# Coarse keys of pairs 12 to 31 held as 126 and 18, the left keys of two pairs handled together

## The chip, the cores and the metric

One NeuronCore of a Trainium2 chip runs the whole program. The metric is the device time of one execution in microseconds, the median of several runs. PE is TensorE, which multiplies matrices; DVE (VectorE), ACT (ScalarE) and POOL (GpSimd) do elementwise work; SP (SyncE) issues most of the transfers. Each engine works through its own instructions in the order in which the program was built.

## What is computed

Eight batches, eight heads, 576 positions, 64 features a head. Attention runs at two scales and the sum of both goes through a gated convolution block:

```python
q_d, k_d, v_d = mean of each 4 neighbouring positions of q, k, v   # 144 coarse positions
out_d  = softmax(q_d k_d^T / 8) v_d                                # coarse attention
out_up = repeat(out_d, 4)
out_local = softmax over |i - j| < 4 of (q k^T / 8), times v       # local attention
x    = out_up + out_local           # [8, 576, 512]
gate = sigmoid(causal depthwise conv of x over 5 positions)
y    = (gate * (x @ w_val)) @ w_out
```

## The kernel before

A **pair** is two heads of one batch on 128 partitions; there are 32, four to a batch, and pair p belongs to batch p // 4. For each pair the coarse part has these steps, each an operation of a planner: `sd` (PE, coarse scores, two pairs at once from pair 8 on), `cmx`, `cbi` (DVE), `cexp` (ACT, exponentials and row sums, into the tile `pd` of 112 query rows x 3 groups x 144 keys), `cgrd`, `crcp` (DVE, the tile `crs` of reciprocals), `cnorm` (multiply `pd` by `crs`, on DVE, POOL or ACT as the planner chooses), `tc0` and `tc1` (PE, lines 948 to 956: the keys are cut in two halves of 72; each half is three transposes of 112 x 72 into a PSUM tile), `pdt0` and `pdt1` (ACT, line 959, copies of these into `pdt`), `odp` (PE, lines 1010 to 1027: two halves x two heads, each a matmul of 72 keys by 64 features over 144 columns, added in PSUM) and `od` (ACT, line 1031, the copy of the result, each value twice). The coarse values come as a sum of four transfers into the tile `vs` of a batch: the first is issued by SP, the three that add to it by POOL, each behind the landing of the one ahead of it.

The local part has `sl` (scores), `mx`, `sub`, `exp`, `sum`, `rcp`, `norm` (tile `pexp`), `tl0`, `tl1` (transposes), `pt`, and `x` (PE, local values). `xt` (DVE) adds both scales into the tile `xt`; `xh`, `xl` split it in two parts for the projections, and four `tap` steps (DVE, line 1070) and `gate` make the convolution gate. The projections go in blocks of 504 positions: `v` (PE, tile `val`), `h` (DVE), `hhi`, `hlo` (the split of h, tile `hhl`), `o` (PE, tile `out`), `ob` (ACT, the scaled copy) and a store by SP. A piece of a projection is three matmuls of 504 columns (lines 1159 to 1161).

The order is made by a planner (`Planner.simulate`) from a hand-written order for PE (`ORDER` up to about pair 12, then the pattern `DOUBLE` for two pairs at a time), durations, and due times; it also decides which engine takes `cnorm`, `norm` and the splits. With `DOUBLE` the even pair's and the odd pair's `odp` stand together, then both `x`, then `tl` of the next pair. PSUM tiles of the kind `t` (for `tl`, `tc`, `odp`) have two buffers. `send` (line 644) holds every SP transfer back until the transfer four ahead of it has landed (`PACE = 4`). `keep_warm` (line 627) puts filler matmuls where the planner expects PE to wait.

Of the kernel before, what the change touches and what calls it, by code (L numbers as in the profile page):

```python
# [86 lines left out]
ROWS, NG, GR = 112, 3, 48  # L87


def scored(p):  # L90

    return p if p < TWOS else p - p % 2
# [104 lines left out]
class Planner:  # L197
# [55 lines left out]
    def switch(self, a, b):  # L253

        a, b = ("P" if "." in k[0] else k[0].rstrip("0123456789") for k in (a, b))
        a, b = self.SHAPE[a], self.SHAPE[b]
# [258 lines left out]
def named(text):  # L515

    name, _, n = text.rpartition(".")
    return name, int(n)


def tensor_order(np_):
# [10 lines left out]
    seq = [named(n) for n in ORDER.split()]  # L532
# [7 lines left out]
    def some(name, p):  # L540
        key = (name, scored(p) if name == "sd" else p)
        if 0 <= p < np_ and key not in seq:
            seq.append(key)
# [21 lines left out]
def tile_two_scale_attn_gated_conv(  # L565
# [6 lines left out]
    vgr: bass.AP,  # L572
    w_val: bass.AP,
# [25 lines left out]
    xhs, xls = (cpool.tile([P, NC, spot(LASTB * S) + S], F32R, name=n) for n in ("xhs", "xls"))  # L599

# [57 lines left out]
    def sums_in(b):  # L658
        u = bt.setdefault(b, {})

        def first(nm, src, shape):
            def run():
                u[nm] = inp.tile(shape, F32, tag=nm, name=f"{nm}{b}", bufs=VSB if nm == "vs" else 2)
                send(out=u[nm], in_=src[b, 0])
            return run

        def more(nm, src, r):
            def run():
                nc.gpsimd.dma_start(out=u[nm], in_=src[b, r], accum_op=ALU.add)
            return run  # L670

        for nm, src, shape, user, size in (
            ("qs", qkr, [P, NC, 2, SD], "sd", P * NC * 2 * SD * 4),
            ("vs", vgr, [VROWS, NC, 4, D], "odp", VROWS * NC * 4 * D * 4),
        ):
# [3 lines left out]
            if nm == "vs":  # L679
                last = NC - 1 + b - VSB  # L680
                free = [(user, last)] if last < NC else [(user, NC * (last - NC + 1) + c) for c in range(NC)]
            op((f"{nm}0", b), "SP", 620, first(nm, src, shape), free=free, size=size)
# [146 lines left out]
    def coarse_scores(p):  # L829
# [62 lines left out]
        def norm(eng):  # L892
            if eng is nc.scalar:
                for g in range(NG):
                    nc.scalar.mul(s["pd"][:, g], s["pd"][:, g], s["crs"][:, g : g + 1])
                return
            return eng.tensor_tensor(
                out=s["pd"], in0=s["pd"], in1=s["crs"].broadcast_to([ROWS, NG, SD]), op=ALU.mult
            )

# [10 lines left out]
        for g, k in enumerate(exps):  # L911
            op(k, "ACT", 356, exp(g), [("cbi", p)] + exps[:g][:1], free=[("tc0", p - 2), ("tc1", p - 2)])
# [29 lines left out]
    def coarse_transpose(p, kb):  # L942
# [17 lines left out]

        op(
# [45 lines left out]
    def coarse_av(p):  # L1007
        s = st[p]

        def mm():  # L1010
# [24 lines left out]

        op(
# [242 lines left out]

    def cw_in():  # L1280
        send(out=cw_raw, in_=conv_w)
# [13 lines left out]
    for p in range(NP):  # L1295
# [9 lines left out]
        coarse_av(p)  # L1305
        conv_split(p)
# [82 lines left out]
```

## Time and profile before

| | |
|---|---|
| median of 3 runs | 368.58 us (368.21 to 369.27) |
| the profiled execution, its own time | 365.61 us |
| span of its trace | 363.8 us |
| PE busy | 354.8 us, 98% |
| DVE, ACT, POOL busy | 311.5, 244.1, 70.3 us |
| granted clock of PE, mean | 0.999 of full speed |
| from 140 to 310 us: PE, DVE busy of 170 us | 169.52, 160.74 us |

The profile shows one execution. Busy times of different engines overlap, so only what stands on the chain that ended last makes the time. Matmuls of PE overlap one another in the trace: what one costs is read from the distance between the starts of the groups on both sides of it, not from its own duration. A float32 matmul leaves two records in the trace, a transpose one.

### The profile page before, as it was taken

To read this page: it belongs to the slowest core of one execution; us is meant where nothing else is said; L and a number is where in the kernel's file an instruction comes from. 1 tells how busy PE (TensorE), PEld (TensorE's weight loads), DVE (VectorE), ACT (ScalarE), POOL (GpSimd) and SP (SyncE) were. 2 spreads that over 40 slices of the span, in tenths; PEclk is the share of its full clock that TensorE was granted. 3 is DMA by queue.
4 is the path that set the end of the run, shared out by engine and by line. 5 is a ranking of instruction groups with operands and counts; after the bars stand their busy time and mean duration, and the time that the engine had idled before them with its cause. 6 is when DMAs were issued, how large, how long until landed. Compare 5 with 4: busy or idle time off the path is not lost.

```text
span 363.8 us, 14500 instructions
## 1 busy us (share of the span) xinstructions
PE 354.8 (98%) x6233; PEld 286.3 (79%) x6233; DVE 311.5 (86%) x696; ACT 244.1 (67%) x658; POOL 70.3 (19%) x95
## 2 busy tenths in 40 slices
PE   8899999999999999999999999999999999999996
PEld 5678776777877788888888887788878787878995
DVE  4999999999999699999999999999998996870520
ACT  2999998977687658784868577676767685422221
POOL 5013252622131123211312031202100110000000
PEclk9999999999999999999999999999999999999999
DMA  8999989999999977995699869992434012002012
GB/s 278 315 286 307 325 226 212 253 254 262 249 229 272 251 243 206 227 264 194 231 206 245 244 183 250 220 266 86 142 125 133 2 41 82 33 0 90 25 49 82
DMA packets 23152, 69.01 MB, mean 190 GB/s; under 512 B 2864, under 2 KB 8240, under 8 KB 23088
## 3 DMA queue, kind: packets, MB, share of 16 engines
q1 hardware_dynamic: 18192, 50.42, 41.6%
q0 software_dynamic: 4608, 17.50, 26.3%
q8 instruction: 49, 0.80, 1.0%
q10 hardware_dynamic: 288, 0.16, 0.2%
q14 instruction: 15, 0.12, 0.1%
HBM read 58.63 MB, written 9.44 MB: 187 GB/s over the span
## 4 chain that ended last, share of the span: by engine, by line
PE 78%; DMA 10%; ACT 6%; DVE 3%; issue 1%; POOL 0%; DVEq 0%; ACTq 0%; POOLq 0%
PE out L1159 9%; PE out L1161 8%; PE out L1160 8%; PE val L1159 8%; PE val L1161 8%; PE val L1160 8%; DMA vs<-in_vgr 7%; PE odp L1021 6%; PE x L979 5%; PE tl L929 5%; PE sl L772 5%; PE tc L952 5%; PE sd L849 3%; DMA out_t<-ob 2%; PE sl L758 1%
## 5 line engine op out<-in xcount | busy, mean ns | idle before, releaser
L1070 DVE SCALAR_TENSOR_TENSOR gp<-xt,cw,gp 128x576 f32<-128x576 f32 x128 | 103.4, 812 | 3.1 <-ACT gp L1064 2.4
L1159 PE MATMUL val<-xhs,wh_v 128*128 128x504 f32 (+1 forms) x160 | 63.0, 394 | 0.0
L1161 PE MATMUL val<-xls,wh_v 128*128 128x504 f32 (+1 forms) x160 | 59.5, 372 | 0.0
L1160 PE MATMUL val<-xhs,wl_v 128*128 128x504 f32 (+1 forms) x160 | 59.4, 371 | 0.0
L1159 PE MATMUL out<-hhl,wh_o 128*128 128x504 f32 (+1 forms) x144 | 58.6, 407 | 0.1
L1161 PE MATMUL out<-hhl,wh_o 128*128 128x504 f32 (+1 forms) x144 | 54.8, 381 | 0.0
L1160 PE MATMUL out<-hhl,wl_o 128*128 128x504 f32 (+1 forms) x144 | 54.7, 380 | 0.0
L872 ACT ACTIVATE pd<-sd,cbi 112x144 f32<-112x144 f32 x96 | 35.5, 387 | 7.8 <-DVE cbi L865 7.8
L1251 ACT ACTIVATE ob<-out 128x504 f32<-128x504 f32 (+2 forms) x40 | 22.1, 557 | 24.4 <-PE out L1161 15.3
L1207 POOL TENSOR_TENSOR hhl<-h,hhl 128x504 fp32r<-128x504 f32 (+1 forms) x17 | 19.3, 1138 | 98.8 <-ACT pt L934 41.9
L1187 DVE SCALAR_TENSOR_TENSOR h<-gp,val 128x288 f32<-128x288 f32 (+6 forms) x64 | 26.6, 445 | 12.8 <-PE val L1161 12.7
L959 ACT COPY pdt<-tc 72x336 f32<-72x336 f32 x64 | 25.5, 434 | 16.3 <-PE tc L952 16.1
L1201 ACT CAST hhl<-h 128x504 fp32r<-128x504 f32 (+2 forms) x44 | 22.0, 521 | 20.3 <-DVE h L1187 19.6
L1161 PEld LDWEIGHTS val<-xls,wh_v 128*128 128x128 f32 x160 | 30.1, 188 | 5.2
L1159 PEld LDWEIGHTS val<-xhs,wh_v 128*128 128x128 f32 x160 | 30.1, 188 | 4.6 <-issue 0.8
L1160 PEld LDWEIGHTS val<-xhs,wl_v 128*128 128x128 f32 x160 | 30.2, 189 | 3.6
L809 DVE TENSOR_TENSOR pexp<-ex,rs 64x350 f32<-64x350 f32 x61 | 31.6, 518 | 1.3
L1081 ACT ACTIVATE gp<-gp 128x576 f32<-128x576 f32 x32 | 22.2, 694 | 14.1 <-DVE gp L1070 14.1
L934 ACT COPY pt<-tl 128x256 f32<-128x256 f32 (+1 forms) x64 | 25.7, 430 | 8.7 <-PE tl L929 8.4
L1161 PEld LDWEIGHTS out<-hhl,wh_o 128*128 128x128 f32 x144 | 27.1, 188 | 5.5 <-DVE hhl L1207 0.4
L1159 PEld LDWEIGHTS out<-hhl,wh_o 128*128 128x128 f32 x144 | 27.1, 188 | 5.4 <-DVE h L1187 0.5
L1160 PEld LDWEIGHTS out<-hhl,wl_o 128*128 128x128 f32 x144 | 27.2, 189 | 3.4
(97 smaller groups left out, 711.9 us busy)
## 6 DMA issues: line engine op xcount, KB each, us to landing
qk<-in_qk SPq DMA_DIRECT2D x32, 586.0 KB, 6.1
qs<-in_qkr POOLq DMA_DIRECT2D x18, 576.0 KB, 7.7
vw<-in_vw SPq DMA_DIRECT2D x32, 320.0 KB, 5.4
out_t<-ob SPq DMA_DIRECT2D x32, 252.0 KB, 5.2
vs<-in_vgr POOLq DMA_DIRECT2D x21, 320.0 KB, 8.2
qs<-in_qkr SPq DMA_DIRECT2D x6, 576.0 KB, 6.6
vs<-in_vgr SPq DMA_DIRECT2D x7, 320.0 KB, 6.7
raw_v<-in_w_val SPq DMA_DIRECT2D x4, 512.0 KB, 5.5
```

Source lines behind the costliest of these rows:

```text
L809: return eng.tensor_tensor(out=px[r].rearrange("p (m b) k -> p b m k", b=2)[:, :, :, BQ * e : BQ * e + KW], in0=s["ex"][r].rearrange("p (b ...
L872: nc.scalar.activation(out=s["pd"][:, g], in_=s["sd"][:, g], func=AF.Exp, scale=1.0 / 128.0, bias=s["bi"][:, g : g + 1], accum_out=s["csm" ...
L934: nc.scalar.copy(out=s["pt"][:, lo : lo + n], in_=s["tl", u])
L959: nc.scalar.copy(out=s["pdt"][:, kb], in_=s["tc", kb])
L1070: return nc.vector.scalar_tensor_tensor(out=s["gp"], in0=s["xt"][:, k : k + S], scalar=cw[:, c, k : k + 1], in1=s["gp"], op0=ALU.mult, op1 ...
L1081: nc.scalar.activation(out=s["gp"], in_=s["gp"], func=AF.Tanh, scale=0.5)
L1159: nc.tensor.matmul(out=o, lhsT=wh[:, d, col], rhs=his[d], start=d == 0, stop=False)
L1160: nc.tensor.matmul(out=o, lhsT=wl[:, d, col], rhs=his[d], start=False, stop=False)
L1161: nc.tensor.matmul(out=o, lhsT=wh[:, d, col], rhs=los[d], start=False, stop=d == NC - 1)
L1187: nc.vector.scalar_tensor_tensor(out=t["h"][:, cs], in0=st[b * NC + c]["gp"][:, f:e], scalar=1.0, in1=box["o"][:, cs], op0=ALU.add, op1=AL ...
L1201: nc.scalar.copy(out=t["hh"][:, cuts[n]], in_=t["h"][:, cuts[n]])
L1251: nc.scalar.mul(t["ob"][:, cs], box["o"][:, cs], 0.5)
```

## The change

From pair 12 on (`PD = 12`) the 144 coarse keys are cut in 126 (`KM`) and 18 (`KR`) instead of 72 and 72.

- The 126 keys of a pair take three transposes (one operation `tc1`; there is no `tc0`). The 18 left keys of each of the three groups are multiplied by `crs` into a small tile (`crest`, on DVE, POOL or ACT): 54 columns for the even pair, 54 for the odd pair, 18 columns of zeros between. One transpose at the odd pair turns all 126 columns. `pdt` becomes one copy of 126 x 336 for the even pair and of 126 x 448 for the odd pair.
- `odp` is one operation for two pairs. First four matmuls of 126 keys by 64 features over 144 columns; then twelve over 48 columns with 54 rows (partitions 0 to 53, even pair) or 62 rows (64 to 125, odd pair) and 64 features, on the four quarters of the array in turn. It needs both buffers of the kind `t`.
- The weights of those twelve stand in a zeroed tile (`spare`, two of them, cleared once on POOL). In it, three transfers for each pair (SP, 18 rows x 128 floats, 9 KB each, from the summed values) lay the left values at the rows of their group: 60 transfers more.
- The sums of values come in two tiles: 126 rows and 18 rows of 512 floats (before 80 rows of 1024). Per batch that is one SP transfer and three POOL transfers more, for batches 3 to 7.

The core of the diff:

```diff
+KM, KR = 126, 18
+PD = 12
...
     def switch(self, a, b):
 
+        rest = a[0] == "odp" and a[1] >= PD and a[1] % 2
...
+    def spread(p):
+        b, c = divmod(p, NC)
+
+        def dma(i):
+            def run():
+                at = 4 * KR * (p % 2) + KR * i
+                send(
+                    out=vzs[p // 2 % 2][at : at + KR, i].rearrange("k h d -> k (h d)"),
+                    in_=bt[b]["vr"][:, P * c : P * c + P],
+                )
+            return run
+
+        for i in range(NG):
+            op((f"vz{i}", p), "SP", 620, dma(i), [("vr3", b), ("zero", 0)], free=[("odp", p - 3 - p % 2)], size=KR * P * 4)
...
+        def rest(eng):
+            at = (NG + 1) * (p % 2)
+            out, in_ = rts[p // 2 % 2][:, at : at + NG], s["pd"][:, :, KM:SD]
...
-        op(("cnorm", p), either(526, 1000, 910), 0, norm, [("crcp", p)], port=BOTH)
+        op(("cnorm", p), either(*((526, 1000, 910) if p < PD else (470, 890, 860))), 0, norm, [("crcp", p)], port=BOTH)
+        if p >= PD:
+            op(
+                ("crest", p), either(140, 300, 600), 0, rest, [("crcp", p), ("zero", 0)],
+                free=[("tc1", p - 3 - p % 2)], port=BOTH,
+            )
...
+        def mm_wide():
+            s["pdt"] = work.tile([KM, n, ROWS], F32, tag="pdt", name=f"pdt{p}")
+            s["tc", 1] = tp = ps.tile([KM, n, ROWS], F32, tag="t", name=f"tc{p}", bufs=TB)
+            keep_warm(tp.rearrange("p a b -> p (a b)"))
+            for i in range(NG):
+                nc.tensor.transpose(
+                    out=tp[:, i],
+                    in_=s["pd"][:, i, 0:KM],
+                    identity=(ident_s if crossed(p, i) else ident)[0:ROWS, 0:ROWS],
+                )
+            if p % 2:
+                nc.tensor.transpose(out=tp[:, NG], in_=rts[p // 2 % 2].rearrange("p g k -> p (g k)"), identity=ident[0:ROWS, 0:ROWS])
...
+        def mm_wide():
+            for x in (p - 1, p):
+                st[x]["odp"] = ps.tile([P, SD], F32, tag="t", name=f"odp{x}", bufs=TB)
...
+                for h, r in enumerate((LO, HI)):
+                    nc.tensor.matmul(
+                        out=st[x]["odp"][r].rearrange("p (i j) -> p i j", j=GR),
+                        lhsT=vd[:, h],
+                        rhs=st[x]["pdt"][:, 0:NG, 64 * h : 64 * h + GR],
+                        start=True,
+                        stop=False,
+                    )
+            for i in range(NG):
+                for x, k in ((p - 1, slice(0, NG * KR)), (p, slice(64, KM))):
+                    for h, r in enumerate((LO, HI)):
+                        q = 64 * (1 - h if crossed(x, i) else h)
+                        nc.tensor.matmul(
+                            out=st[x]["odp"][r, GR * i : GR * i + GR],
+                            lhsT=vzs[p // 2 % 2][k, i, h],
+                            rhs=s["pdt"][k, NG, q : q + GR],
+                            start=False,
+                            stop=i == NG - 1,
+                        )
```

Because durations and operations change, the planner also orders some work anew, from about pair 8 on. On PE the pieces between the attention steps stay nearly the same; three filler matmuls appear ahead of `tc` of pair 8. `cnorm` goes to DVE 11 times instead of 16, to POOL 5 times instead of once, to ACT 16 times instead of 15; `crest` goes to ACT 12 times, to POOL 5 times, to DVE 3 times. `norm` of pairs 17 and 25 goes from DVE to POOL.

PE at the coarse transposes of pair 15, before: `tc15_1` and `tc15_0` are the two halves, `out2` a piece of the output projection.

```order
L1161 MATMUL out2_1_2990<-hhl2_1_2759,wh_o_98 128x504
L952 MATMUL tc15_1_3025<-ident_s_78,pd15_2801 72x112 x2
L952 MATMUL tc15_1_3025<-ident_77,pd15_2801 72x112
L952 MATMUL tc15_0_3029<-ident_s_78,pd15_2801 72x112 x2
L952 MATMUL tc15_0_3029<-ident_77,pd15_2801 72x112
L1159 MATMUL out2_0_2917<-hhl2_2_2888,wh_o_98 128x504
```

The same place now; `spare1` is the small tile with the left keys of pairs 14 and 15.

```order
L1277 MATMUL out2_1_3018<-hhl2_1_2778,wh_o_98 128x504
L1023 MATMUL tc15_3057<-ident_s_78,pd15_2823 126x112 x2
L1023 MATMUL tc15_3057<-ident_77,pd15_2823 126x112
L1029 MATMUL tc15_3057<-ident_77,spare1_1719 126x112
L1275 MATMUL out2_0_2947<-hhl2_2_2930,wh_o_98 128x504
```

Six transposes have become four (three at an even pair), between the same pieces.

PE at the weighted values of pairs 12 and 13, before, behind a piece of `val2`:

```order
L1161 MATMUL val2_3_2812<-xls_90,wh_v_96 128x504
L1021 MATMUL odp12_2821<-pdt12_2471,vs3_1436 64x144 x4
L1021 MATMUL odp13_2826<-pdt13_2649,vs3_1436 64x144 x4
L979 MATMUL x12_2835<-pt12_2567,vw12_2173 64x58 x20
L979 MATMUL x13_2857<-pt13_2762,vw13_2549 64x58 x20
L929 MATMUL tl14_1_2884<-ident_77,pexp0_80 128x128 x2
```

The same place now:

```order
L1277 MATMUL val2_3_2834<-xls_90,wh_v_96 128x504
L1098 MATMUL odp12_2842<-pdt12_2572,vs3_1257 64x144 x2
L1098 MATMUL odp13_2843<-pdt13_2672,vs3_1257 64x144 x2
L1109 MATMUL odp12_2842<-pdt13_2672,spare0_1717 64x48 x2
L1109 MATMUL odp13_2843<-pdt13_2672,spare0_1717 64x48 x2
L1109 MATMUL odp12_2842<-pdt13_2672,spare0_1717 64x48 x2
L1109 MATMUL odp13_2843<-pdt13_2672,spare0_1717 64x48 x2
L1109 MATMUL odp12_2842<-pdt13_2672,spare0_1717 64x48 x2
L1109 MATMUL odp13_2843<-pdt13_2672,spare0_1717 64x48 x2
L1060 MATMUL x12_2866<-pt12_2589,vw12_2356 64x58 x20
L1060 MATMUL x13_2889<-pt13_2781,vw13_2578 64x58 x20
```

Four matmuls over 144 columns have gone and twelve over 48 have come; what stands ahead and behind is the same.

SP's queue at the stores of block 3, before (`out_t` is the result, `ob3` a block of it):

```order
L644 DMA out_t<-ob3_0_3781 128x504
L644 DMA out_t<-ob3_1_3834 128x504
L644 DMA qk23_3854<-in_qk 128x1172
L644 DMA out_t<-ob3_2_3917 128x504
L644 DMA vw21_3982<-in_vw 128x640
L644 DMA vw22_3995<-in_vw 128x640
L644 DMA out_t<-ob3_3_4021 128x504
```

The same place now:

```order
L653 DMA out_t<-ob3_0_3826 128x504
L653 DMA out_t<-ob3_1_3879 128x504
L653 DMA spare0_1717<-vs5_2863 18x128 x6
L653 DMA vw21_4064<-in_vw 128x640
L653 DMA qk23_4086<-in_qk 128x1172
L653 DMA out_t<-ob3_2_3978 128x504
L653 DMA out_t<-ob3_3_4081 128x504
```

Six small transfers now stand between the second and the third store, and such a row of six (or the six in two or three parts) stands in the queue once for every two pairs.

## Rows read from the trace of the kernel before

**Rows 1.** Page, part 1: busy us, share of the span, instructions of each engine.

```profile
PE 354.8 (98%) x6233; PEld 286.3 (79%) x6233; DVE 311.5 (86%) x696; ACT 244.1 (67%) x658; POOL 70.3 (19%) x95
```

**Rows 2.** Windows, 140 to 310 us: PE, PEld, DVE, ACT, POOL busy; clock, DMA share, GB/s.

```profile
140.00:310.00 170.00, 169.52 (x3263) 138.09 (x3262) 160.74 (x363) 120.43 (x327) 29.06 (x30) 1.00 0.64 174
```

**Rows 3.** Timeline of PE, six coarse transposes: start us, us, engine, line, tiles, count.

```profile
204.79 0.40 PE L1161 MATMUL val<-xls,wh_v 128*128 128x504 f32 x1
205.03 0.35 PE L952 MATMUL tc<-ident_s,pd 112*72 112x112 f32 x2
...
205.85 0.39 PE L1160 MATMUL val<-xhs,wl_v 128*128 128x504 f32 x1
```

**Rows 4.** Timeline of PE, three coarse transposes of one half.

```profile
89.39 0.39 PE L1160 MATMUL val<-xhs,wl_v 128*128 128x504 f32 x1
89.61 0.39 PE L1161 MATMUL val<-xls,wh_v 128*128 128x504 f32 x1
89.84 0.26 PE L952 MATMUL tc<-ident_s,pd 112*72 112x112 f32 x1
...
90.38 0.39 PE L1160 MATMUL val<-xhs,wl_v 128*128 128x504 f32 x1
```

**Rows 5.** Timeline of PE, `odp` and `x` of two pairs, then `tl`.

```profile
214.41 1.20 PE L1021 MATMUL odp<-pdt,vs 72*64 72x144 f32 x16
215.54 1.39 PE L979 MATMUL x<-pt,vw 64*64 64x58 f32 x80
216.86 0.77 PE L929 MATMUL tl<-ident,pexp 128*128 128x128 f32 x5
217.38 0.48 PE L1159 MATMUL val<-xhs,wh_v 128*128 128x504 f32 x1
```

**Rows 6.** Timeline of PE, `odp` and `x` of one pair alone.

```profile
83.28 0.71 PE L1021 MATMUL odp<-pdt,vs 72*64 72x144 f32 x8
83.92 0.81 PE L979 MATMUL x<-pt,vw 64*64 64x58 f32 x40
84.65 0.50 PE L1159 MATMUL out<-hhl,wh_o 128*128 128x504 f32 x1
```

**Rows 7.** Timeline of PE, `sd`: 144 columns on quarters of the array.

```profile
209.37 0.97 PE L849 MATMUL sd<-qs 64*64 64x144 f32 x24
```

**Rows 8.** Groups of PE by shape, fillers at `tc`: count, busy us, mean ns, idle before.

```profile
L627 PE MATMUL tc<-const-bfloat16-1.0 128*72 128x336 bf16 x13 | 2.5, 308 | 0.4 <-ACT pt L934 0.4
```

**Rows 9.** Groups of ACT by shape: the copy `pdt`, and a narrow operation.

```profile
L959 ACT COPY pdt<-tc 72x336 f32<-72x336 f32 x64 | 25.5, 434 | 16.3 <-PE tc L952 16.1
L1106 ACT ACTIVATE cw_low<-cw_raw 128x20 uint16<-128x20 uint32 x1 | 0.2, 227 | 0.0
```

**Rows 10.** Groups of DVE by shape: `cnorm`.

```profile
L897 DVE TENSOR_TENSOR pd<-pd,crs 112x432 f32<-112x432 f32 x16 | 9.7, 613 | 0.2
```

**Rows 11.** Timeline of DVE at the last pairs.

```profile
309.59 1.56 DVE L990 TENSOR_TENSOR xt<-x,od 128x290 f32<-128x290 f32 x4 [3.00 <-PE x L979]
```

**Rows 12.** Waits: engine, line, waited for, us in total, times, longest us.

```profile
POOL vs L669 <- DMA vs<-in_vgr: 40.8, 14, 5.5
```

**Rows 13.** Timeline of DVE: the reciprocals of pairs 22 and 23.

```profile
216.59 0.24 DVE L890 RECIPROCAL crs<-cs 112x3 f32<-112x3 f32 x2
```

**Rows 14.** The chain of waits: start us, us, engine, tile: `tc` of pair 22, a store.

```profile
114.17 7.44 DMA out_t<-ob
121.69 0.59 ACT ob L1251
...
222.16 0.58 PE tc L952 x6
```

**Rows 15.** Timeline of PE behind that store.

```profile
122.70 0.71 PE L1021 MATMUL odp<-pdt,vs 72*64 72x144 f32 x8 [0.42 <-ACT pt L934]
```

**Rows 16.** DMA issues: count, KB each, median us from issue to landing.

```profile
out_t<-ob SPq DMA_DIRECT2D x32, 252.0 KB, 5.2
out_t<-ob SPq DMA_DIRECT2D x7, 144.0 KB, 1.8
```

More of the change, by code (lines that the diff above doesn't have):

```diff
@@ L541, in some @@
         key = (name, scored(p) if name == "sd" else p)
+        if p >= PD and (name == "tc0" or name == "odp" and p % 2 == 0):
+            return
         if 0 <= p < np_ and key not in seq:
@@ L659, in sums_in, with main @@
         u = bt.setdefault(b, {})
+        wide = NC * b >= PD
+        def main(nm):
+            return u[nm][:, 0 : NC * P] if nm == "vs" and wide else u[nm]
         def first(nm, src, shape):
             def run():
-                u[nm] = inp.tile(shape, F32, tag=nm, name=f"{nm}{b}", bufs=VSB if nm == "vs" else 2)
-                send(out=u[nm], in_=src[b, 0])
+                if nm == "vr":
+                    u[nm] = u["vs"][0:KR, NC * P :]
+                else:
+                    u[nm] = inp.tile(shape, F32, tag=nm, name=f"{nm}{b}", bufs=VSB if nm == "vs" else 2)
+                send(out=main(nm), in_=src[b, 0])
             return run
@@ L673, in sums_in @@
             ("qs", qkr, [P, NC, 2, SD], "sd", P * NC * 2 * SD * 4),
-            ("vs", vgr, [VROWS, NC, 4, D], "odp", VROWS * NC * 4 * D * 4),
-        ):
+            ("vs", vmr, [KM, 2 * NC * P], "odp", KM * NC * P * 4)
+            if wide
+            else ("vs", vgr, [VROWS, NC, 4, D], "odp", VROWS * NC * 4 * D * 4),
+            ("vr", vrr, None, "odp", KR * NC * P * 4),
+        ):
+            if nm == "vr" and not wide:
+                continue
             if nm == "qs" and b < SUMB:
@@ L959, in evac, with evac_wide @@
             nc.scalar.copy(out=s["pdt"][:, kb], in_=s["tc", kb])
+        n = NG + p % 2
+        def mm_wide():
[10 more added lines that the diff above has]
+                nc.tensor.transpose(out=tp[:, NG], in_=rts[p // 2 % 2].rearrange("p g k -> p (g k)"), identity=ident[0:ROWS, 0:ROWS])
+        def evac_wide():
+            nc.scalar.copy(out=s["pdt"], in_=s["tc", 1])
+        if p >= PD:
+            if kb:
+                op(
+                    ("tc1", p), "PE", 99 * n, mm_wide, [("cnorm", p)] + [("crest", x) for x in (p - 1, p) if p % 2],
+                    banks=[("t", [("pdt1", p)])], cols=(196 * n, 336), loads=n,
+                )
+                op(("pdt1", p), "ACT", 335 + 95 * (p % 2), evac_wide, [("tc1", p)], free=[("odp", p - 2 if p < PD + 2 else (p - 2) | 1)])
+            return
         op(
@@ L1034, in evac @@
             )
+        if p >= PD:
+            if p % 2:
+                op(
+                    ("odp", p), "PE", 915, mm_wide,
+                    [("vs3", p // NC)] + [(n, x) for x in (p - 1, p) for n in ("pdt1", "vz0", "vz1", "vz2")],
+                    banks=[("t", [("od", x)]) for x in (p - 1, p)], cols=(1152, 144), loads=32,
+                )
+            op(("od", p), "ACT", 299, evac, [("odp", p | 1)], free=[("xt0", p - 2), ("xt1", p - 2)])
+            return
         op(
@@ L1277, in out_unit, with zero @@
         op((f"od{c}", j), "SP", 620, dma(slice(0, split), send), [(f"ob{c}", j)], size=P * split * 4)
+    def zero():
+        n, done = NG * 2 * D, []
+        for i, tag in enumerate(("a", "bits")):
+            t = stage.tile([P, 512], F32, tag=tag, name=f"spare{i}", bufs=1)
+            done.append(nc.gpsimd.memset(t, 0.0))
+            vzs.append(t[0:KM, 0:n].rearrange("k (g h d) -> k g h d", g=NG, h=2))
+            rts.append(t[0:ROWS, n : n + (2 * NG + 1) * KR].rearrange("p (g k) -> p g k", k=KR))
+        return done
+    op(("zero", 0), "POOL", 1500, zero, [("wlo", 2 * NC - 1)], port=("POOL",))
     def cw_in():
@@ L1372 @@
         ("vgr", vgr),
+        ("vmr", vmr),
+        ("vrr", vrr),
         ("w_val", wv),
```

35 lines of the change are left out of this document (27 added, 8 removed).

## The prediction

> **What bounds the kernel now.** I read the busy times first, then the windows, then the timeline of PE, then the waits. PE is busy for 354.8 us of the span [rows 1], and in the stretch in which pairs 12 to 31 do their coarse work, 140 to 310 us, for 169.52 of 170 us at the full clock (2.4 GHz) [rows 2]. A busy PE may still be a stretched one, so the timeline decides: the starts of its groups follow one another without a hole [rows 3 to 6]. PE therefore sets the pace, and what is taken from it there counts in full until another engine is late. The nearest other engine is DVE, busy for 160.74 us of the same 170 [rows 2]; 3.00 of its 9.26 idle us are one wait for PE, for `x` of the last pairs [rows 11]. ACT has 49.6 us to spare, POOL 140.9 [rows 2].
>
> **Transposes on PE.** Costs are distances between starts. One matmul of a projection stands 0.22 or 0.23 us ahead of the next start (89.39, 89.61, 89.84 [rows 4]); I use 0.23. Six transposes between two pieces: 204.79 to 205.85 is 1.06 us, less two steps of 0.23, so 0.60 [rows 3]. Three: 89.61 to 90.38 is 0.77, less 0.46, so 0.31 [rows 4]. Each further one is then 0.29/3 = 0.097 us. After the change the even pair pays 0.31 and the odd one, with four, 0.41: 0.72 instead of 1.20 for two pairs, a gain of 0.48. The new transposes have 126 columns of weights, not 72; the five of `tl` with 128 take 0.52 us, 0.104 each, though over 128 columns [rows 5]. At that price seven cost 0.05 more, gain 0.43. I keep 0.48, because what streams stays 112 wide.
>
> **Weighted values on PE.** `odp` of two pairs takes 214.41 to 215.54, 1.13 us for 16 records [rows 5]; one pair alone 0.64 for 8 [rows 6]. So 8 records are 0.49 and 0.15 is fixed. The new form keeps 8 records of 144 columns (0.49) and the fixed 0.15, and has 24 records of 48 columns on four quarters. The trace has no such row; the nearest is `x`, 58 columns on four quarters: 80 records in 1.32 us [rows 5], 40 in 0.73 [rows 6], so 14.8 ns for each further one, 16.5 with everything. Scaled by columns 24 would cost 0.29, unscaled at most 0.40. The far end is `sd`, 144 columns on quarters, 0.97/24 = 40 ns a record [rows 7], which would be 0.97. Nothing in it can be below nothing, as 24 records are issued. I take 0.33, near `x`. New: 0.15 + 0.49 + 0.33 = 0.97, a gain of 0.16 (0.09 to 0.20). The change between halves and quarters of the array happened between `odp` and `x` and now happens inside `odp`, so it is paid once as before.
>
> The Trainium skill has a rule against this step: TensorE: Matmul & The Clock Gate, section "Wait — 56ns, not 53.3ns?", says that matmuls never start closer than about 25 ns, however few columns they have. By it the 24 records would be 0.60 us, and `odp` would lose 0.11 instead of gaining 0.16. The rows of `x` stand at 16.5 ns, so in this form the trace does not agree.
>
> **Sum on PE.** 0.48 + 0.16 = 0.64 us for two pairs; pairs 12 to 31 are ten of these: 6.4 us.
>
> **What takes some of it back.** (1) Three fillers ahead of `tc` of pair 8: the planner expects PE to wait there. By their row 13 of them took 2.5 us [rows 8], so three cost 0.6; a wait of the same size may remain beside them, or the wait would have been there anyway: 0 to 1.0, I take 0.6. (2) `odp` now hands both results over at once, and needs both buffers of the kind `t`; `tl` of the next pair needs them back after `x`, 1.32 us later [rows 5]. ACT must make two copies in that time (`pdt`, a copy of like size, is 434 ns [rows 9]): it fits where ACT is free, and costs PE some 0.2 us where ACT has just begun something else. I take 0.4 for all ten, bounds 0 and 2. Behind the waiting `tl` the projections' pieces are queued, so such a wait is paid in full.
>
> **Edits priced at nothing.** DVE has 5 of 16 `cnorm` of 613 ns [rows 10] fewer, 9 of those left are narrower by an eighth, and 3 narrow `crest` come, at less than half a `cnorm` each: 3.1 + 0.7 - 0.9, about 3 us less, and four `norm` fewer beside. That is less than PE gains, but the idle 9.26 us [rows 2] is cover, and the 3.00 us wait shrinks with PE. ACT loses 40 copies `pdt` of 434 ns for 20 of a third more width at most, some 7 us, and gets 36 narrow products at up to 227 ns [rows 9], 8.2 us: even. POOL gets 15 accumulating transfers, 5 `crest` and 4 more `cnorm`; it has room [rows 2]. If that cover goes, the rivals below are what it costs. Bytes hardly change: the sums carry a tenth less, the 60 small transfers 0.55 MB more, and the transfers' share of that stretch is 0.64 [rows 2].
>
> 6.4 - 0.6 - 0.4 = 5.4 us. The profiled execution took 365.61 us, its span 363.8; the runs' median is 368.58. I take the gain from both alike: 360.2 for a profiled execution, **363.2** for the median.
>
> **Rival 1, quarters that do not overlap as they do in `x`.** Even and odd pair read different rows of one tile and write different buffers, as both halves of `x` do, which speaks against it; the twelve matmuls add onto results just written, which `x` doesn't do. If only two run at a time, a slot is a third of an `odp` slot (0.49/4 x 48/144 = 0.041 us [rows 5, 6]), twelve are 0.49, `odp` gains nothing, and 4.8 - 1.0 = 3.8 us remain: 364.8. At 25 ns a record, as above, it would be 0.37 for two pairs, 2.7 us in all and 365.9.
>
> **Rival 2, POOL's queue.** `cnorm` of pairs 20, 23, 26, 28 and `norm` of 17 and 25 now stand on POOL behind transfers that each wait for the landing of the one before. POOL waited so 14 times, 40.8 us, 2.9 on average and 5.5 at most [rows 12]. Between the reciprocals at 216.59 [rows 13] and `tc` of the pair at 222.16 [rows 14] lie 5.6 us, so an average wait plus some 0.9 for the product hides and the longest is 0.8 late. Six such places, each 0.8 to 1.5 when the shorter round has eaten some of the slack: 5 to 9 us in the worst case, 3 in a middling one: 366.2 to 368.6.
>
> **Rival 3, on the other side: stores behind the small transfers.** Only four SP transfers are under way at once, and six new ones stand in a row ahead of stores and loads, once for two pairs. A short store lands in 1.8 us, a usual one in 5.2 [rows 16]; the second wave of a row begins when the first has landed, so the next store is some 3.6 us late. The trace shows the mechanism: a store of 7.44 us holds an `ob` of ACT [rows 14], and PE idles 0.42 us behind it [rows 15]. A late `ob` keeps the projection's PSUM buffer. At 0.42 us for each of ten rows the gain falls to 1.2; from 0.54 it is gone; at twice 0.42 the kernel is 3.0 slower: 371.6. Against it: the planner puts the loads early, and one such stall is all that the trace has.
>
> The Trainium skill, DMA: Bandwidth & Descriptors, section "Rules for kernel authors", says to gather small transfers in a large one, since below 64 KB mostly overhead is paid. That speaks for this rival: these carry 9 KB. No row here has one so small.
>
> **Chances.** The forecast (361.2 to 364.6) 0.66; rival 1 0.11; rival 2 0.12; rival 3 0.11. A measurement of this kernel can tell about 0.3% (1.1 us) from no change. The forecast, rival 1 and about a third of rival 2 are faster by more: 0.81. Most of the rest of rival 2 is within it, and the mild end of rival 3: 0.10. Slower 0.09. The range leaves out rival 3's far end and reaches over rival 2: 361.0 to 368.6.
>
> **What the profile after would show.** Steps right: `tc` of an odd pair takes about 0.41 us between pieces, of an even one 0.31; `odp` of two pairs 0.97 from its start to `x`; the distance from one `odp` of two pairs to the next shrinks by 0.64; PE stays busy. Wrong: `odp` over 1.1 (rival 1); holes ahead of `tc` or `tl` with POOL as releaser (rival 2); holes ahead of projections with ACT `ob` and a store behind it (rival 3); or PE idle at `h` and `x`, which would say that DVE has become the bound.

## The result, and the profile after

The changed kernel takes 365.59 us (median of 22 runs), the kernel before beside it 366.76: a ratio of 0.9918, 95% interval 0.9889 to 0.9947, or 3.0 us less. Run again on another occasion it took 365.07 beside 366.88, 0.9951 (0.9920 to 0.9982). The forecast was 5.4 us less, a ratio of 0.985: the sign was right, and of the gain about half came the first time and a third the second. Both medians lie in the whole range (361.0 to 368.6) but above the forecast's own band (361.2 to 364.6), although the kernel before itself came out 1.8 us under the 368.58 from which the forecast was taken; from 366.76 the same gain would give 361.4. By the time alone rival 1 (364.8 to 365.9) would fit better, so only the profiles tell what happened. Medians are over all runs of a kernel while ratios leave out those that lie over 1.5% above its fastest (9 of these 22 of the changed kernel, all with a granted clock of 0.981 to 0.995), and since the first profile of the changed kernel is of one of these, the rows of after below are those of the second profile of the same kernel.

Part 1 of the page of the changed kernel, in answer to [rows 1]:

```profile
PE 351.1 (97%) x6346; PEld 282.9 (78%) x6346; DVE 305.6 (84%) x692; ACT 246.2 (68%) x677; POOL 91.3 (25%) x123
```

PE is busy for 3.7 us less, not the 6.4 of the sum. The windows say where. The columns are busy time of PE with its instructions, granted clock, DMA share, GB/s; first the changed kernel, then the kernel before in a second profile (the run e5_before_again below), which lies at its median:

```profile
0.00:60.00 60.00, 55.07 (x1224) 1.00 0.96 280
60.00:140.00 80.00, 77.50 (x1422) 0.98 0.92 228
140.00:310.00 170.00, 170.00 (x3414) 1.00 0.68 185
310.00:362.10 52.10, 48.52 (x291) 0.99 0.14 48
```

```profile
0.00:60.00 60.00, 55.88 (x1230) 1.00 0.94 282
60.00:140.00 80.00, 78.91 (x1464) 1.00 0.98 249
140.00:310.00 170.00, 168.42 (x3178) 1.00 0.64 173
310.00:365.20 55.20, 51.59 (x381) 0.99 0.15 50
```

From 140 us on, PE of the changed kernel does not idle at all ([rows 2] had 0.48 us of idle time, the second profile of before 1.58). The same window with all engines (PE, PEld, DVE, ACT, POOL) shows that the cover for the edits priced at nothing held: DVE hardly moved, ACT has 4.7 us more, POOL has a quarter of the stretch.

```profile
140.00:310.00 170.00, 170.00 (x3414) 137.52 (x3413) 161.15 (x372) 125.11 (x356) 42.89 (x51) 1.00 0.68 185
```

The rounds themselves are as forecast. Timeline of PE of the changed kernel, `odp` and `x` of pairs 14 and 15 (in answer to [rows 5]):

```profile
161.19 0.71 PE L1098 MATMUL odp<-pdt,vs 126*64 126x144 f32 x8
161.83 0.56 PE L1109 MATMUL odp<-pdt,spare 54*64 54x48 f32 x24
162.21 1.35 PE L1060 MATMUL x<-pt,vw 64*64 64x58 f32 x80
163.50 0.77 PE L984 MATMUL tl<-ident,pexp 128*128 128x128 f32 x5
```

From `odp` to `x` are 1.02 us: 0.64 for the wide records, 0.38 for the 24 narrow ones. The transposes of an odd pair, between two pieces (in answer to [rows 3, 4]):

```profile
224.94 0.39 PE L1277 MATMUL out<-hhl,wh_o 128*128 128x504 f32 x1
225.17 0.36 PE L1023 MATMUL tc<-ident_s,pd 112*126 112x112 f32 x2
...
225.46 0.26 PE L1029 MATMUL tc<-ident,spare 112*126 112x112 f32 x1
225.49 0.47 PE L1275 MATMUL out<-hhl,wh_o 128*128 128x504 f32 x1
225.80 0.39 PE L1276 MATMUL out<-hhl,wl_o 128*128 128x504 f32 x1
```

224.94 to 225.80 is 0.86, less two steps of 0.23: 0.40. `odp` of pairs 14 and 15 starts at 161.19, that of pairs 28 and 29 at 289.24: seven rounds of 18.29 us, where the kernel before has 18.97 (19.10 in its second profile). So 0.68 us or more is gained in a round, for a sum of 0.64. The starts, in the changed kernel:

```profile
142.90 0.71 PE L1098 MATMUL odp<-pdt,vs 126*64 126x144 f32 x8
...
289.24 0.71 PE L1098 MATMUL odp<-pdt,vs 126*64 126x144 f32 x8
```

and in the first profile of before, with the first start of its second one behind them:

```profile
138.74 1.20 PE L1021 MATMUL odp<-pdt,vs 72*64 72x144 f32 x16
...
157.62 1.20 PE L1021 MATMUL odp<-pdt,vs 72*64 72x144 f32 x16
...
290.40 1.20 PE L1021 MATMUL odp<-pdt,vs 72*64 72x144 f32 x16
...
138.58 1.20 PE L1021 MATMUL odp<-pdt,vs 72*64 72x144 f32 x16
```

The loss lies ahead of pair 12. `odp` of pairs 12 and 13 starts at 142.90 us; in the two profiles of before at 138.74 and 138.58. From there to the end the changed kernel needs 219.2 us, before 225.1 and 226.6: on the average of these 6.6 us won behind that point, 4.2 lost in front of it. PE's timeline has one large hole there, at `tc` of pair 8, the place of the three fillers:

```profile
90.66 0.59 PE L636 MATMUL tc<-const-bfloat16-1.0 128*72 128x336 bf16 x3 [1.47 <-ACT pt L989]
91.54 0.40 PE L1007 MATMUL tc<-ident_s,pd 112*72 112x112 f32 x1 [0.29 <-ACT pd L933]
...
92.23 0.77 PE L1275 MATMUL val<-xhs,wh_v 128*128 128x504 f32 x1
```

Both releasers are ACT. What ACT does there (the small rows that read an accumulator, one behind each `pd`, are left out):

```profile
84.89 0.38 ACT L910 ACTIVATE pd<-sd,cbi 112x144 f32<-112x144 f32 x1 [0.56 <-DVE cbi L903]
...
87.83 0.59 ACT L1367 ACTIVATE ob<-out 128x504 f32<-128x504 f32 x1 [2.47 <-DMA out_t<-ob]
...
89.74 0.40 ACT L910 ACTIVATE pd<-sd,cbi 112x144 f32<-112x144 f32 x1
...
90.10 0.51 ACT L989 COPY pt<-tl 128x384 f32<-128x384 f32 x1
...
91.03 1.06 ACT L933 ACTIVATE pd<-pd,crs 112x144 f32<-112x144 f32 x3
```

Between the first and the second of the six `pd` of pairs 8 and 9 stands an `ob`, and it waits 2.47 us for an earlier store to land before it may fill its buffer again. Five `pd`, a `pt`, `xhs` and the product `pd` that `tc` reads are queued behind it. The kernel before has such a wait too, 2.34 us at 121.69 [rows 14], but there only 0.42 us of it reach PE [rows 15]; at pair 8 its `ob` stands behind all six `pd` and waits for nothing:

```profile
86.12 0.41 ACT L872 ACTIVATE pd<-sd,cbi 112x144 f32<-112x144 f32 x1
...
87.04 0.64 ACT L1251 ACTIVATE ob<-out 128x504 f32<-128x504 f32 x1
```

The first profile of the changed kernel has the same `ob` between the first and the second `pd`, with 1.66 us of wait, and 0.92 us of idle time on PE in front of the fillers.

Then the hole costs a second time. Windows of PE in the changed kernel:

```profile
88.00:90.00 2.00, 1.06 (x89) 1.00 1.07 353
90.00:92.00 2.00, 1.05 (x5) 0.89 1.07 228
92.00:94.00 2.00, 2.00 (x7) 0.50 1.02 325
94.00:96.00 2.00, 2.00 (x9) 0.76 0.93 273
```

PE is idle for 1.9 us of the first four, and the granted clock falls to 0.50 (1.2 GHz) behind it: the `val` at 92.23 takes 0.77 us where one at full clock takes 0.48. Until it is back, about 1.7 us are lost (an estimate: the share of the clock that is missing in these windows, times 2 us each).

In the first profile the clock fell at another place: to 0.50 behind 2.17 us of idle time at an `odp` 59 us into the program that waits for the landing of a sum of values, while it stayed at 1.00 at `tc` of pair 8.

### The profile page after: what moved, and what is told of

The parts are those of the page before. It is cut to its first block, busy times and chain, and to the rows that moved or that the text cites. A ratio compares the mean times of both kernels' runs of the same rounds, so it can differ in the third digit from the quotient of the medians.

```text
span 364.2 us, 14850 instructions
## 1 busy us (share of the span) xinstructions
PE 351.6 (97%) x6346; PEld 282.5 (78%) x6346; DVE 306.6 (84%) x692; ACT 245.8 (67%) x677; POOL 91.3 (25%) x123
## 4 chain that ended last, share of the span: by engine, by line
PE 67%; DMA 18%; DVE 7%; ACT 4%; issue 1%; POOL 1%; SPq 0%; DVEq 0%; ACTq 0%
DMA vs<-in_vgr 9%; PE out L1275 8%; PE out L1277 8%; PE out L1276 8%; PE val L1275 7%; PE val L1277 7%; PE val L1276 7%; PE tl L984 4%; PE sl L810 4%; PE x L1060 4%; DMA out_t<-ob 3%; DMA qk<-in_qk 3%; PE sd L887 3%; DVE gp L1186 2%; DMA vg<-in_vg 2%; PE tc L1023 2%
## 5 line engine op out<-in xcount | busy, mean ns | idle before, releaser
L1275 PE MATMUL val<-xhs,wh_v 128*128 128x504 f32 (+1 forms) x160 | 63.8, 398 | 0.0
L1323 POOL TENSOR_TENSOR hhl<-h,hhl 128x504 fp32r<-128x504 f32 (+1 forms) x15 | 17.8, 1193 | 58.4 <-DVE pexp L847 27.2
L1071 DVE TENSOR_TENSOR xt<-x,od 128x290 f32<-128x290 f32 x64 | 26.2, 447 | 5.7 <-PE x L1060 3.2
L847 DVE TENSOR_TENSOR pexp<-ex,rs 64x350 f32<-64x350 f32 x57 | 29.9, 524 | 1.1
```

The source lines that it names most:

```text
L847: return eng.tensor_tensor(out=px[r].rearrange("p (m b) k -> p b m k", b=2)[:, :, :, BQ * e : BQ * e + KW], in0=s["ex"][r].rearrange("p (b ...
L1071: nc.vector.tensor_tensor(out=s["xt"][:, 4:].rearrange("p (m a j r) -> p a m j r", m=NPR, a=2, r=2)[:, par], in0=s["x"][par].rearrange("p ...
L1275: nc.tensor.matmul(out=o, lhsT=wh[:, d, col], rhs=his[d], start=d == 0, stop=False)
```

## The experiments

Theory A after this reading: the rounds give what was forecast, and the rest is lost in front of pair 12, where the new transfers and the new order come among the work of pairs 7 to 11. Theory B: the rounds or the end of the program give half of the gain back, because the transfers or the narrow records cost more than their sum.

**The changed kernel again** (no edit), for a second profile:

> The changed kernel once more, for an undisturbed execution. Theory A (the ten rounds give the 0.64 us each that was forecast, and about 3 us of it are lost ahead of pair 12, where the planner's order and the transfers changed too): ratio to the kernel before 0.992; odp of pairs 12 and 13 starts 2 to 4 us later than 138.7, rounds from one odp of two pairs to the next of 18.3 instead of 18.95. Theory B (nothing is lost early, a round gives only half of what was forecast, or the tail gives it back): the same ratio, odp of pairs 12 and 13 within 0.5 us of 138.7, rounds of 18.6 or more, or PE idle behind pair 31.

365.07 us, 0.9951; rounds of 18.29 us, and the hole at `tc` of pair 8. So the profile is as A has it: what is missing lies in front. The end of the program is the same in both (3.6 us of PE's last 52 to 55 are idle, in the windows above).

**The new form from pair 16 on:**

```diff
-PD = 12
+PD = 16
-    op(("zero", 0), "POOL", 1500, zero, [("wlo", 2 * NC - 1)], port=("POOL",))
+    op(("zero", 0), "POOL", 1500, zero, [("wlo", 2 * NC - 1), ("crcp", 13)], port=("POOL",))
```

> The split only from pair 16 on, and the clearing of the weights' tiles held back until the reciprocals of pair 13, so that the order of PE ahead of pair 16 is that of the kernel before. Eight double pairs instead of ten. Theory A: 8 x 0.63 = 5.0 us, ratio 0.986, faster than the changed kernel although it does less of the change; odp of pairs 12 and 13 at 138.7 within 1. Theory B: eight tenths of the 3.0 us measured, 2.4 us, ratio 0.9935, slower than the changed kernel.

365.03 us, 0.9939 (0.9909 to 0.9970): eight rounds of ten, yet about 2.2 us. Its rounds are 18.3 us as well, but it too comes late to them: `odp` of pairs 14 and 15, still in the old form, starts at 160.69, in the two profiles of before at 157.62 and 158.18. One loss can be read. Timelines of DVE, POOL and PE of this kernel:

```profile
107.76 2.56 DVE L935 TENSOR_TENSOR pd<-pd,crs 112x432 f32<-112x432 f32 x1
```

```profile
107.58 0.82 POOL L686 DMA_DIRECT2D vs<-in_vrr  x1 [0.61 <-ACT pdt L1014]
108.13 1.71 POOL L1323 TENSOR_TENSOR hhl<-h,hhl 128x252 fp32r<-128x252 f32 x2
```

```profile
114.30 0.41 PE L984 MATMUL tl<-ident,pexp 128*128 128x128 f32 x2 [1.23 <-DVE pexp L847]
```

A new accumulating transfer stands on POOL's queue in front of two pieces of `hhl`; these run beside a `cnorm` on DVE, and that takes 2.56 us instead of the usual 0.61 [rows 10]. `pexp` comes late, and PE waits 1.23 us. That reads like rival 2's queue, at another place and with another price, but it is one profile and no run took it away: that the transfer is what made `hhl` late is not shown. The Trainium skill, GPSIMD Engine Reference, section "Specifications", says that POOL's way to SBUF is shared with VectorE and that DVE instructions with two inputs in SBUF contend for it. The trace agrees: this product has two, and is stretched fourfold.

**The fourth batch's sums of values, in both tiles, and the clearing held back** (the first edit moves their due times by 4 or 8 us, the second makes the clearing wait for pair 10; the two were not tried apart):

```diff
-    ... tap2.11:+1500"
+    ... tap2.11:+1500 vs0.3:+8000 vr0.3:+8000 vr1.3:+8000 vr2.3:+8000 vr3.3:+8000 vs1.3:+4000 vs2.3:+4000 vs3.3:+4000"
-    op(("zero", 0), "POOL", 1500, zero, [("wlo", 2 * NC - 1)], port=("POOL",))
+    op(("zero", 0), "POOL", 1500, zero, [("wlo", 2 * NC - 1), ("crcp", 10)], port=("POOL",))
```

> The whole change, but the first sums of batch 3 made due 4 to 8 us later and the clearing held back until the reciprocals of pair 10, so that the order ahead of pair 12 stays nearer to the kernel before and no filler is added. Theory A: most of the loss is gone, 5 to 6.3 us, ratio 0.983 to 0.986. Theory B: ratio 0.992 as the changed kernel.

361.93 us, 0.9874 (0.9837 to 0.9912): about 4.6 us less than before, and beside the changed kernel's 0.9951 on the same chip the intervals do not touch (beside its first 0.9918 they do). Rounds of 18.28, `odp` of pairs 12 and 13 at 141.24. The planner's order there has the `ob` behind the six `pd` again. So the form of the rounds was never the difference.

**The transfers alone, with the old work on PE** (before, plus a second small sum for each batch from the fourth on and three small copies for each pair from 12 on; the two cleared tiles are left out of the diff; PE reads nothing of it):

```diff
+            op(("vr0", b), "SP", 620, left0, [("vs0", b)], free=[...], size=size)
+            for r in range(1, FAC):
+                op((f"vr{r}", b), "POOL", 960, left(r), [(f"vr{r - 1}", b)], size=size)
...
+        for i in range(NG):
+            op((f"vz{i}", p), "SP", 620, dma(i), [("vr3", b), ("zero", 0)], free=[("odp", p - 3 - p % 2)], size=KR * P * 4)
```

> The kernel before with the change's additional transfers and clearing, but the old work on PE: from batch 3 on a second small sum (80 x 112 floats, four transfers, about the same bytes as the 18 rows), two cleared tiles and three transfers of 18 x 112 floats for each pair, which odp waits for in the plan and nobody reads. Theory A: it pays what the changed kernel loses ahead of pair 12 and gains nothing: 2 to 4 us slower, ratio 1.006 to 1.011. Theory B: the transfers are hidden, ratio 1.000 within 0.003. Rival 3 of the prediction (stores behind the small transfers): PE idle behind late ob copies between 140 and 310 us, 4 us and more there.

371.98 us, 1.0154 (1.0101 to 1.0206): 5.6 us slower. Its rounds from pair 14 to pair 28 are 18.82 to 19.64 us, on average 19.09, at most 0.1 above before; in its profile what is lost is in front: `odp` of pairs 12 and 13 comes at 143.14. Windows of its PE:

```profile
88.00:90.00 2.00, 0.18 (x22) 0.07 (x10) 0.90 (x3) 2.00 (x10) 1.42 (x2) 1.00 1.07 307
90.00:92.00 2.00, 1.77 (x5) 1.23 (x6) 2.00 (x6) 2.00 (x8) 0.80 (x1) 0.57 1.04 240
```

(PE, PEld, DVE, ACT and POOL busy, then clock.) A hole at the same place, with ACT busy throughout, behind an `ob` that waited 1.74 us for a store; and the same fall of the clock. It is not the same to the row: here the `ob` stands ahead of all six `pd`, and PE waits 2.05 us at a `val` for `xhs`. A hole of this kind thus needs none of the new work on PE.

**The kernel before again** (no edit):

> The kernel before, once more, as a second profile of it. Both theories: a median of 366.9 us as its other runs on this chip, ratio 1.000 within its interval, rounds of 18.97 us from pair 14 to pair 28. It tells how far the start of odp of pairs 12 and 13 scatters between two profiles of one kernel: if it lies between 138 and 140 us again, the 2.5 to 4.2 us by which the changed kernels come there later are theirs; if it comes at 142 us or later, most of that is scatter of the first 140 us.

367.14 us, 0.9995 (0.9969 to 1.0022); `odp` of pairs 12 and 13 at 138.58. The 4.2 us are not scatter between the two profiles of the kernel before; how far two profiles of a changed kernel scatter is seen further down.

**The transfers alone, held back:** the kernel of the transfers alone (three small copies for each pair, six for two), with the two edits that hold the fourth batch back.

> The kernel before with the second sums, the cleared tiles and the six small transfers of each pair from 12 on, as in the run of the transfers alone, but with those of the fourth batch and the clearing put later (behind crcp of pair 10, as in the version that holds them back); the order on PE ahead of pair 12 is then that of before except for one sd. Theory A (what is lost is lost where these come among the work of pairs 7 to 11): no hole at tc of pair 8, granted clock 1.00 from 80 to 100 us, and only the 0.1 us a round that the run of the transfers alone showed: 367 to 368.5 us. Theory B (the transfers cost the time themselves, wherever they stand): 371 to 372 us as that run.

369.6 us, 1.0060 (1.0026 to 1.0094), 2.2 us: between the two theories. Of the 5.6 us that the transfers cost, 3.4 go with their place and the order made around it. The other 2.2 stay with them at this second place. Where these lie in a usual execution is not known: the only profile is of an execution of 373.18 us, 3.6 above the median. It has no hole at `tc` of pair 8, but one in the rounds. ACT and PE there:

```profile
241.28 0.59 ACT L1289 ACTIVATE ob<-out 128x504 f32<-128x504 f32 x1 [4.08 <-DMA out_t<-ob]
```

```profile
242.22 0.55 PE L966 MATMUL tl<-ident,pexp 128*128 128x128 f32 x3 [3.28 <-ACT od L1068]
```

An `ob` waits 4.08 us for a store, an `od` stands behind it, and `tl` waits for that `od`; the clock is at 0.50 from 244 to 246 us, and this one round takes 23.9 us. This is what rival 3 and term (2) of the prediction describe, and small transfers stand on SP in front of the stores issued last before it and behind them. Whether they are what delays the store, and how often it happens, is not shown.

**Eight more fillers at the hole:**

```diff
+TC8 = 0
...
+            if (p, kb) == (8, TC8):
+                plan.warm = 8
+                keep_warm(tp.rearrange("p a b -> p (a b)"))
```

> The changed kernel, with eight more fillers (128x336 bf16, 0.20 us each, 1.6 us) in front of the first tc of pair 8; every other instruction and its order as in the changed kernel. If the hole at this tc pulls the clock down and the lower clock costs as much as the hole again (val of 0.77 us for 0.48 behind it): granted clock 1.00 in 90 to 96 us, mean clock 0.998 or more in most runs, and about 363.5 us, 1.5 us under the changed kernel. If the clock falls for another reason: as the changed kernel, 365 us, with 0.50 in 92 to 94 us. If the hole is not there in most runs: 1.0 to 1.6 us slower than the changed kernel.

365.9 us, 0.9931 (0.9893 to 0.9968): no gain that can be told. The fillers could not fill the hole, since they write the buffer that `tc` waits for. Timeline of PE:

```profile
91.86 1.75 PE L637 MATMUL tc<-const-bfloat16-1.0 128*72 128x336 bf16 x11 [2.45 <-ACT pt L990]
```

ACT has the `ob` between two `pd` here too, this time with 3.19 us of wait. The clock stayed at 1.00 through 2.45 us of idle time, so a hole of this size does not always pull it down; what it saved went into the fillers. Over the twelve executions the fillers did not keep the clock up: seven have a mean of 0.995 or less.

**Without the narrow records** (the version that is held back; the share of the 18 left keys in `odp` is left out):

```diff
-            for i in range(NG):
-                for x, k in ((p - 1, slice(0, NG * KR)), (p, slice(64, KM))):
...
-                        stop=False,
+                        stop=True,
```

> The version that holds the fourth batch's second sums back, without the 24 matmuls of 48 columns of each two pairs (the share of the 18 left keys in odp is left out), so that odp of two pairs has its 8 wide matmuls alone. If the rounds are bound by PE and the 24 records cost 16 ns each, as they do from record to record: a round falls from 18.28 to 17.90 us, and the time from 361.9 to 358.1 us. If another engine or a transfer ends the rounds: a round of 18.2 us or more and over 361 us.

0.9781 (0.9709 to 0.9854), so about 359.0 us, from only two compared executions; the rounds are the better measure, read from the profile, at full clock:

```profile
165.75 0.71 PE L1098 MATMUL odp<-pdt,vs 126*64 126x144 f32 x8
...
291.77 0.71 PE L1098 MATMUL odp<-pdt,vs 126*64 126x144 f32 x8
```

Seven rounds from pair 14 to pair 28 take 126.02 us, 18.00 each instead of 18.28. So the 24 records are on the path, at 0.28 us a round: of their 0.38 us 0.03 come back at `x` (1.32 us for 1.29), and the other 0.07 were not followed. PE sets the length of a round: from 140 to 310 us it idles 0.29 us in all.

**One `ob` moved.** The reading above names one instruction of ACT. This kernel is the changed one, with the fourth `ob` of the first block emitted behind the six `pd`, the `pt` and the `xhs`; every other engine's order is the changed kernel's, row for row. What moved on ACT, as a difference of its order:

```diff
-ACTIVATE pd8,csm8<-sd8,cbi8 112x144
-ACTIVATE ob0<-out0 128x504
-ACTIVATE pd8,csm8<-sd8,cbi8 112x144
+ACTIVATE pd8,csm8<-sd8,cbi8 112x144 x2
...
+ACTIVATE ob0<-out0 128x504
```

> The changed kernel with one instruction moved: the fourth ob of the first block, which waits for the landing of an earlier store between the first and the second pd of pairs 8 and 9, comes on ACT behind the sixth pd, the pt and the xhs, about where the kernel before has it; every other engine's order is the same to the row. Theory A (ACT held by this ob is what opens the hole at tc of pair 8, and the hole is what pulls the clock down): PE idle in 86 to 96 us 0.5 us or less for 1.9, granted clock 1.00 there, odp of pairs 12 and 13 near 139.5 us for 142.9, and 365.1 - 1.5 - 1.7 = about 362 us, ratio 0.987. Theory B (the store's landing is late for the new transfers, and whatever stands behind it waits as long): the hole comes back one step later, at the second tc of pair 8 or at odp, and the time stays at 364.5 to 365.5 us, ratio 0.993 to 0.995.

362.71 us, 0.9882 (0.9828 to 0.9936). Timeline of ACT, and windows of PE, in this kernel:

```profile
85.99 0.40 ACT L917 ACTIVATE pd<-sd,cbi 112x144 f32<-112x144 f32 x1
...
86.34 0.51 ACT L996 COPY pt<-tl 128x384 f32<-128x384 f32 x1
86.70 0.72 ACT L1172 CAST xhs<-xt 128x576 fp32r<-128x576 f32 x1
87.28 0.63 ACT L1374 ACTIVATE ob<-out 128x504 f32<-128x504 f32 x1
```

```profile
88.00:90.00 2.00, 2.00 (x37) 1.00 1.00 244
90.00:92.00 2.00, 2.00 (x16) 1.00 1.01 225
```

The store has landed by the time the `ob` comes, and nothing waits. PE is never idle from 84 to 96 us, the clock stays at 1.00, and `odp` of pairs 12 and 13 starts at 138.71. The same kernel once more:

> The changed kernel with the one ob behind the six pd, once more. If that one position took what the changed kernel lacks of the forecast: no PE idle over 0.5 us at tc of pair 8, granted clock 1.00 from 80 to 100 us, ratio between 0.985 and 0.990 again (362 to 363.5 us). If its first run was a lucky sample: 364.5 us or more, ratio 0.993, with the hole back.

364.03 us, 0.9906 (0.9868 to 0.9943). PE does not wait at `tc` of pair 8 in this profile either, so the cause of that hole is shown twice. But the time is short of what was expected, and `odp` of pairs 12 and 13 starts at 142.84, 4.1 us later than in the first profile of this same kernel. It has two other early holes, 1.51 us at a `tc` of an earlier pair and 1.42 us at `x` of pair 7, and the clock fell behind the first (windows of PE below). The `ob` ahead of the one that was moved waits 1.59 us for a store in this profile, 0.24 in the first: the wait moves from one `ob` to another between executions. Whether it brought the hole at `x` is not shown; the profile names no releaser there.

```profile
50.00:52.00 2.00, 1.39 (x6) 1.00 1.04 240
52.00:54.00 2.00, 2.00 (x7) 0.59 1.05 247
54.00:56.00 2.00, 2.00 (x46) 0.55 0.81 117
```

**The version that is held back, with its third `ob` moved** behind the `ex` and the `gp` that follow it on ACT:

```diff
-ACTIVATE ob0<-out0 128x504
...
+ACTIVATE ob0<-out0 128x504
```

> The version that holds the fourth batch's second sums back, with the third ob of the first block (2.85 us of wait for a store at 84.2 us in its profile, in front of the ex of pair 8 and a gp) put behind these two on ACT; every other order the same. Theory A: ex of pair 8 starts at once, pexp comes 2 us or more earlier, the wait of 1.03 us at tl of pair 8 (88.8 us) goes, and 361.9 - 0.9 = about 361 us, ratio 0.984 to 0.985. Theory B: what follows the moved ob is then late in its turn, and the time is that of the version without the move, 361.9, ratio 0.987.

362.55 us, 0.9886 (0.9837 to 0.9934), beside the version without the move:

> The version that holds the fourth batch's second sums back once more, on the same chip as the two others: both theories 361.9 us, ratio 0.987, rounds of 18.28 us and odp of pairs 12 and 13 between 140.5 and 142 us.

361.50 us, 0.9853 (0.9803 to 0.9903). The wait at `tl` of pair 8 (1.03 and 0.87 us in two profiles without the move) is gone with it, but the time is not better: a wait of a microsecond here is less than two executions of one kernel can differ by in their first 140 us (`odp` of pairs 12 and 13 starts at 141.24 and 142.97 in the two profiles without the move). B for this one. The version that is held back has the lowest ratios of all, 0.9874 and 0.9853, better than both kernels; the versions with an `ob` moved (0.9882 to 0.9906) cannot be told from it.

## Why the prediction was right, and where its sum was off

**What bounds the kernel: right.** In the stretch of the rounds PE is busy for 170.00 of 170 us, and leaving out 24 records shortens each round by 0.28 us.

**Transposes: right.** 0.41 forecast for the odd pair, 0.40 measured; 0.31 for the even one, 0.30 between the pieces at 223.27 and 224.03 (0.76 less 0.46). The 126 columns of weights cost nothing, as I had chosen.

**`odp`: right within its bounds.** 0.38 for the narrow records against 0.33 (bounds 0.29 to 0.40), 1.02 against 0.97. That is 16 ns a record, the price of `x` with everything, not of `x` scaled by columns. The gain is 0.11, not 0.16; `x` gives 0.03 back. By the rule of the Trainium skill quoted in the prediction (TensorE: Matmul & The Clock Gate, section "Wait — 56ns, not 53.3ns?") they would have taken 0.60 us; the trace does not agree in this form, four quarters of the array side by side. That counts every record as a matmul, as the prediction did. A float32 matmul of the program leaves two, and counted by these twelve they stand 32 ns apart, which the rule allows; `sl`, whose 80 records (40 matmuls) take 0.81 us from 148.75 to 149.56 in this profile, stands under it by either count, at 20 ns a matmul.

**The sum of a round: right.** 0.64 forecast, 0.68 or more measured from round to round, and the small waits of before in this stretch (0.48 us of idle time in [rows 2], 1.58 in its second profile), which are gone, are enough for the surplus.

**What takes some of it back, (2): not there.** I took 0.4 for `tl` waiting for `od`, bounds 0 to 2. In the changed kernel PE has no idle time from 140 to 310 us: 0. The wait exists, though: the transfers alone, held back, had one of 3.28 us.

**What takes some of it back, (1): the term that failed.** I had the place, `tc` of pair 8, and gave it 0.6 us, at most 1.0. The row of fillers after, in answer to [rows 8]:

```profile
L636 PE MATMUL tc<-const-bfloat16-1.0 128*72 128x336 bf16 x16 | 3.1, 307 | 2.0 <-ACT pt L989 1.7
```

The fillers are the 0.6 us. Beside them stand 1.76 us of waits and about 1.7 us at the low clock, so that this place costs some 4 us in that profile. I had priced the wait by the planner's fillers, which are its guess of a wait, and had not followed `tc` back on ACT. There the order had changed: an `ob` that must wait for a store had come in front of five `pd`. With it moved back, both profiles lose this hole. I had the mechanism itself in hand, in rival 3 with [rows 14, 15], and tied it to the small transfers of the rounds, not to ACT's order in front of them. Nor did the sum have any term for the clock.

How often the clock falls can be counted. In the runs that the ratios compare, 65 of 70 of the kernel before have a mean granted clock of 0.998 or more, and 11 of 23 of the changed one, the others 0.991 to 0.995. Half a per cent of 365 us is 1.8 us, in half of the runs: about 0.9 us of the missing 2.4, an estimate. The times bear it out roughly: those 11 take 363.7 us on average, the other 12 take 365.0. Of all its 34 executions the changed kernel has 23 with the lower clock. Which hole it fell behind is known for the two profiled ones alone, `tc` of pair 8 in one and an earlier `odp` in the other, so these 0.9 us are not the price of one hole.

**The rivals.** 1, quarters that do not overlap: false, 1.02 where it wanted over 1.1. 2, POOL's queue: not in the rounds, where no hole has POOL as its releaser. In the kernel that begins at pair 16 a wait of 1.23 us in front of the rounds reads like it; no run took it away. 3, stores behind the small transfers: not in the rounds of the changed kernel, though one such stall stands in the rounds of the transfers alone, held back. Its mechanism, an `ob` that holds ACT, is what opened the hole in front, without the small transfers of the rounds: the first of them is issued at 100.68 us, behind the hole.

**What stays open.** With the one `ob` moved the kernel reached 0.9882 and 0.9906, against 0.9918 and 0.9951 with it where it was. The direction is the same both times, but the intervals overlap, and the start of its rounds lay at 138.71 and 142.84 us, so the worth of that one position is not settled; the hole and its cause are. Medians over all executions point the same way, 365.59 and 365.07 us with the `ob` where it was, 362.71 and 364.03 with it moved. That what is missing lies in front of the rounds does not hang on it: held back, the whole change reached 0.9874 and 0.9853, about the forecast's 0.985. In the first 60 us PE idles 4.1 us in both profiles of before, 7.2 and 4.9 in the changed kernel's two, 5.4 and 5.7 with the `ob` moved, 6.4 and 5.4 in the version that is held back, although no queue's order differs before 54 us. Why, two profiles of before cannot say. And where the 2.2 us lie that the transfers alone cost even when held back is not known; the one profile of it is of an unusually long execution.

## What to carry to other kernels

When a change makes the planner reorder work, follow each engine's queue in front of the changed stage, not only the engine that sets the pace: an instruction that waits for a DMA (here a copy that reuses a store's buffer) holds all that is queued behind it, and one place earlier it can stand in front of the path. Price a hole on PE as idle time, and allow as much again for the work done at the low clock that may follow it. And add transfers where the queues have room: issued later, with the order planned around that, the same transfers cost 3.4 us less.

## What the hardware showed that was not expected

- The granted clock fell to 0.5 to 0.6 (the lower level is 1.2 GHz) for some 4 us behind holes of 1.76 us and 2.17 us (the changed kernel, second and first profile), 1.51 us (with the `ob` moved, second profile) and 2.05 us (the transfers alone), and did not fall behind 2.45 us (with more fillers) or 1.42 us. Executions of one kernel differ in it: a mean clock of 0.998 or more in 11 of 34 of the changed one.
- 24 records (twelve matmuls) of 48 columns on the quarters of the array, adding onto results just written, take 16 ns each, as much as those of 58 columns that only write.
- A product on DVE with two inputs in SBUF went from 0.61 to 2.56 us while two products of 1.71 us together ran on POOL (one case).
